# Placing the three turns of a weight conversion within a pair of attention heads

## The chip, the cores and the metric

The kernel runs on one core of a Trainium2 chip. Its time is the device time of one execution in microseconds (us). Before the change it is 1604.77 us, the median of three runs (1603.15 to 1604.81).

## What is computed

The program is an attention layer with normalised queries and keys, followed by a gated feed-forward layer. Cut to what matters:

```python
# q, k, v: (8 sequences, 12 heads, 448 positions, 64); float32
rmsnorm = lambda x, g: x / sqrt(mean(x*x, -1) + 1e-6) * g
scores  = 1/8 * rmsnorm(q, g_q) @ rmsnorm(k, g_k).T
attn    = softmax(scores)
x       = (attn @ v), heads side by side            # (3584, 768)
xn      = x / sqrt(mean(x*x, -1) + 1e-6) * rms_g
out     = (silu(xn @ w_gate) * (xn @ w_val)) @ w_out   # weights float64 -> float32
```

The three weight matrices arrive as float64 and have to become float32 on the chip, in 72 pieces. That is the conversion which the change is about.

## The kernel before

Heads are worked on in pairs: 6 pairs to a sequence (`NPAIR`), 48 in all (`NG`). Each engine runs its own instructions in the order in which the program states them. `pe(fn)` states one step of TensorE work and then whatever was put off with `after(n, ...)` until `n` such steps later. So the place of a call in the text is its place in every engine's stream.

Pair 0 and pairs 1 to 6 (`g <= NPAIR`) run alone, before there is any feed-forward work to lie beside. In these, the parts concerned are:

```python
raw_pool, cv_pool = pool("c_raw", 7), pool("c_cv", 4)
ps_s, ps_m, ps_f = 4, 1 and 3 banks of PSUM
...
def squares(g, i):                      # sums of squares of q (i = 0) or k (i = 1)
    nc.scalar.activation(sq, st["qk", g][:, i], ACT.Square)              # L478
    after(1, reduce)                    # VectorE tensor_reduce            L481
    ...
    elif i == 1:
        after(2, lambda: rms_qk(g))     # GpSimd add, pow                  L497, L498
        after(2, lambda: norm_q(g))     # GpSimd multiply x2               L503

def turn(g, i):                         # transposes of q (i = 0) or k (i = 1)
    ...                                 # TensorE                          L519, L523
    if i == 0:
        nc.scalar.activation(st["qT", g], ps, ACT.Copy, scale=gqk)        # L524
        nc.vector.tensor_copy(st["kT", g][:, LAST], ps[:, S:])            # L525
    else:
        nc.vector.tensor_copy(st["kT", g][:, FULL], ps[:, FULL])          # L527

def score(g, cs):                       # for each chunk c and head j
    ps = ps_s.tile(...); nc.tensor.matmul(ps, kT, qT)                     # L537
    nc.scalar.activation(e, ps, ACT.Exp, scale=rs)                        # L541

def rests(g):                           # the last 64 positions
    nc.tensor.matmul(...)               # scores of pair g                 L567
    av = ps_m.tile(...)                 # the only bank of ps_m
    nc.tensor.matmul(av, ...)           # values of pair g-1, first term   L573
    nc.tensor.matmul(den, ones, e)      # denominators of g-1, first term  L578
    nc.scalar.activation(e, ps, ACT.Exp)                                  # L582

def values(g):  nc.tensor.matmul(av, vt, e)      # 6 of them               L589

def sums(g):
    nc.tensor.matmul(den, ones, e)      # 6 of them                        L602
    nc.vector.reciprocal(rd, den)                                         # L606
    nc.vector.tensor_tensor(x, av, rd, ALU.mult)                          # L617
    ...                                 # later: ScalarE square L620/L622, GpSimd sum L623
```

The conversion moves one step on with each call of `convert()`, a turn. One turn works on several pieces at different stages, with `n` the number of the turn:

```python
def convert():
    ...
    if 0 <= n - 5 < len(pieces):        # last stage of piece n-5
        nc.gpsimd.tensor_tensor(w, top, lo, ALU.add)                      # L773
    if 0 <= n - 4 < len(pieces):        # join of piece n-4: three on VectorE
        nc.vector.tensor_scalar(top, top, 122879.99, 2.0**-15, ...)       # L734
        nc.vector.tensor_scalar(top, top, 3, 0x3FFFFFF8, ...)             # L735
        nc.vector.scalar_tensor_tensor(top, hi, -(2**30), top, ...)       # L736
    if 0 <= n - 3 < len(pieces):        # split of piece n-3: two on ScalarE
        top = cv_pool.tile(...)         # one of 4 buffers
        nc.scalar.activation(top, hi, ACT.Abs)                            # L728
        nc.scalar.activation(lo, lo, ACT.Copy, scale=2.0**-29)            # L729
    if n < len(pieces):                 # load of piece n into one of 7 raw buffers
        st["raw", n] = load_raw(pieces[n][1])                             # L719
    if 0 <= n - 7 < len(pieces):        # piece n-7 is put away in DRAM
        keep(pieces[n - 7][0])                                            # L761
```

A `top` buffer is written by the split (L728) and read for the last time by the GpSimd addition (L773) of the same piece, two turns later.

Of the kernel before, what the change touches and what calls it, by code (L numbers as in the profile page):

```python
# [22 lines left out]
NPAIR = H // 2  # L23
# [312 lines left out]
def safe_scores(  # L336
# [45 lines left out]
    def pe(fn):  # L382
        now["t"] += 1
        fn()
        for item in [d for d in due if d[0] <= now["t"]]:
            due.remove(item)
            item[1]()
# [15 lines left out]
    def load_pair(g):  # L403

        if g >= NG:
            return
        b, hp = divmod(g, NPAIR)
        qk = st["qk", g] = qk_pool.tile([128, 2, 2 * NK * D], F32, name="qk")
        nc.sync.dma_start(out=qk[:, 0].rearrange("p (h n) -> p h n", h=2),
                          in_=q[b, 2 * hp:2 * hp + 2, FULL].rearrange("h (p t) d -> p h (t d)", t=NK))  # L410
        for h in range(2):
            nc.sync.dma_start(out=qk[:, 1].rearrange("p (t h d) -> p h t d", h=2, d=D)[:, 1 - h],
                              in_=k[b, 2 * hp + h, FULL].rearrange("(p t) d -> p t d", t=NK))

    def load_v(g):
        if g >= NG:
            return
        b, hp = divmod(g, NPAIR)
        vt = st["v", g] = v_pool.tile([128, 2, NK, D], F32, name="vt")
        nc.sync.dma_start(out=vt.rearrange("p h t d -> p h (t d)"),  # L420
                          in_=v[b, 2 * hp:2 * hp + 2, FULL].rearrange("h (p t) d -> p h (t d)", t=NK))


    def load_rests(b, i, engine):
        if b >= B:
            return
        if i == 0:
            st["rest", b] = rest_pool.tile([128, NPAIR, 2, D], F32, name="rest")
        for h in range(2):
            engine.dma_start(out=st["rest", b][own(i), :, 1 - h], in_=(q, k)[i][b, h::2, LAST].rearrange("h i d -> i h d"))  # L430

    def load_v_rests(b):
        if b >= B:
            return
        vr = st["vr", b] = rest_pool.tile([128, NPAIR, D], F32, name="vr")
        for h in range(2):
            nc.sync.dma_start(out=vr[across(h)], in_=v[b, h::2, LAST].rearrange("h i d -> i h d"))
# [91 lines left out]
    def score(g, cs):  # L529

        qT, kT, rs = st["qT", g], st["kT", g], st["rs", g]
        sc = {}
        for c in cs:
            for j in range(2):
                r = across(j)
                ps = sc[c, j] = ps_s.tile([128, 512], F32, name="sc", tag="s")
                nc.tensor.matmul(ps[:, 0:S], lhsT=kT[r, c * 128:(c + 1) * 128], rhs=qT[r, :], start=True, stop=True)  # L537
        for (c, j), ps in sc.items():
            e = st["e", g, c, j] = e_pool.tile([128, S], F32, name="e")
            n = 2 * NK + c * 2 + 1 - j  # L540
            nc.scalar.activation(e, ps[:, 0:S], ACT.Exp, scale=rs[:, n:n + 1])  # L541


        def first():
            for j in range(2):
                es = st["es", g, j] = tmp.tile([128, S], F32, name="es", tag="es", bufs=4)
                nc.gpsimd.tensor_tensor(es, st["e", g, 0, j], st["e", g, 1, j], ALU.add)  # L547

        def more(of):
            for j in range(2):  # L550
                r = across(j) if of == "rest" else slice(0, 128)
                e = st["e", g, of] if of == "rest" else st["e", g, of, j]
                es = st["es", g, j]
                nc.gpsimd.tensor_tensor(es[r], es[r], e[r], ALU.add)  # L554

        if NK - 1 in cs and not direct(g):
            n = 3 if g == NPAIR + 1 else 2
            after(n, first)
            after(n + 2, lambda: more(2))
            after(n + 3, lambda: more("rest"))  # L560
# [202 lines left out]
    def convert():  # L763

        n = turn_of["n"]
        if n >= TURNS or not room(1):
            return False
        turn_of["n"] += 1
        if 0 <= n - 5 < len(pieces):
            key = pieces[n - 5][0]  # L770
            st[key] = block()
            lo, top = st.pop(("cv", n - 5))
            nc.gpsimd.tensor_tensor(data(key).bitcast(I32), top, lo, ALU.add)  # L773
        if 0 <= n - 4 < len(pieces):
            st["cv", n - 4] = join(*st.pop(("cv", n - 4)))
        if 0 <= n - 3 < len(pieces):
            st["cv", n - 3] = split(st.pop(("raw", n - 3)))
        if n < len(pieces):
            st["raw", n] = load_raw(pieces[n][1])
        if 0 <= n - 7 < len(pieces):  # L780
            keep(pieces[n - 7][0])
        if turn_of["n"] == TURNS:

            free_w.extend(cv_pool.tile([128, BW], F32, name="top") for _ in range(2))
            whole = [raw_pool.tile([128, 2 * BW], F32, name="raw") for _ in range(7)]
            room_so.extend(whole[:6])
            homes = [whole[6][:, 0:BW], whole[6][:, BW:]] + [cv_pool.tile([128, BW], F32, name="top") for _ in range(2)]
            carried.extend(t[:, i * 128:(i + 1) * 128] for t in homes for i in range(3))
        return True
# [421 lines left out]
    def load_rows():  # L1211
        nc.sync.dma_start(out=rg, in_=moe_rms_g.rearrange("(c p) -> p c", p=128))
        nc.sync.dma_start(out=row[:, 0, :], in_=g_q.rearrange("(o d) -> o d", o=1))
        nc.sync.dma_start(out=row[:, 1, :], in_=g_k.rearrange("(o d) -> o d", o=1))
# [20 lines left out]
    def turns(n):  # L1235

        for _ in range(n):
            convert()
# [14 lines left out]
    for g in range(NG + 1):  # L1253
        b, hp = divmod(g, NPAIR)
        if g:
            load_pair(g + 3)
        if hp == 2:
            for i in range(2):
                load_rests(b + 1, i, nc.sync)
            load_v_rests(b + 1)  # L1260
        if g == 0:
            pe(lambda: score(0, (0,)))
            pe(lambda: rests(0))
            pe(lambda: score(0, (1, 2)))
            pe(lambda: turn(1, 0))
            squares(2, 0)
            squares(2, 1)
            pe(lambda: turn(1, 1))
            norm_rests(0, 2, 4)
            for _ in range(3):  # L1270
                convert()
            load_pair(3)
            load_v(2)
            convert()
            load_rows()
            continue
        if g <= NPAIR:
            pe(lambda: score(g, (0,)))
            squares(g + 2, 0)
            squares(g + 2, 1)  # L1280
            turns(g < NPAIR)
            if g > 1:
                pe(lambda: turn(g + 1, 0))
                some_rests(g)
                pe(lambda: turn(g + 1, 1))
            pe(lambda: rests(g))
            pe(lambda: values(g - 1))
            if g == 1:
                pe(lambda: turn(g + 1, 0))
                some_rests(g)  # L1290
                pe(lambda: turn(g + 1, 1))
            load_v(g + 2)
            turns(g < NPAIR)
            pe(lambda: sums(g - 1))
            pe(lambda: score(g, (1, 2)))
            turns(1 if g < NPAIR else 3)
            if g == 2:
                bound()
            continue

        pe(lambda: (rests(g), score(g, (0,)) if g < NG else None))
        if g == NPAIR + 1:
            pe(lambda: rms_x(0))
        pe(lambda: values(g - 1))
        load_v(g + 2)
        if g == NPAIR + 1:
            pe(lambda: score(g, (1,)))
            pe(lambda: norm_x(0))
            pe(lambda: score(g, (2,)))
        pe(lambda: sums(g - 1))  # L1310
        if g == NPAIR + 1:
            begin(0, 15)
        elif g < NG:
            pe(lambda: score(g, (1, 2)))
        st["block"] = now["t"]
        if hp:
            fill()
            squares(g + 2, 0)
            squares(g + 2, 1)
            pe(lambda: turn(g + 1, 0))  # L1320
            some_rests(g)
            fill()
            pe(lambda: turn(g + 1, 1))
            fill()
            continue
        fill(3)
        pe(lambda: turn(g + 1, 0))
        fill(1)
        pe(lambda: rms_x(b - 1))
        squares(g + 2, 0)  # L1330
        squares(g + 2, 1)
        pe(lambda: turn(g + 1, 1))
        fill(len(todo))
        begin(b - 1, 16)
        pe(lambda: norm_x(b - 1))
        fill()
# [41 lines left out]
```

## Time and profile before

| | before |
|---|---|
| time, median of 3 | 1604.77 us |
| span of the profiled execution | 1601.2 us |
| TensorE busy | 1574.3 us (98%) |
| VectorE busy | 879.0 us (55%) |
| ScalarE busy | 469.9 us (29%) |
| GpSimd busy | 658.7 us (41%) |

In the profile PE is TensorE, DVE VectorE, ACT ScalarE, POOL GpSimd and SP the engine that issues the transfers. L773 is line 773 of the kernel. The busy share of TensorE takes in time in which a matrix product was issued and waited in the pipeline, so it is not a measure of how near the engine is to its peak. A row of the timeline gives the start in us from the start of the span, the duration in us, the engine, line and operation, what is written and read, the count, and in square brackets how long the engine stood idle before it and what ended that. The duration of one instruction runs a little past the start of the next on the same engine; where a stream is without gaps, the time that an instruction takes up is the distance between starts.

The pairs that run alone fill about the first 100 us of the span; the conversion lasts until 280 us.

### The profile page before, as it was taken

The numbers are of one execution on the slowest core, as the hardware profiler recorded it, in microseconds if no ns is written. First come the engines' busy times: TensorE is split into PE (matmuls) and PEld (weight loads), VectorE is DVE, ScalarE is ACT, GpSimd is POOL, SyncE is SP. The second block draws the span as 40 slices with busy tenths as digits, with TensorE's granted clock in tenths as the row PEclk, the third lists the DMA queues.
The fourth block names the chain that finished last, engine by engine and source line by source line (L and its number), as shares of the span: only waits on it lengthen the run. The fifth ranks groups of instructions, "written<-read, shape, count | busy, mean of one in ns | idle before, by whom it ended". The sixth has DMA issues, their size and how long they took to land.

```text
span 1601.2 us, 21577 instructions
## 1 busy us (share of the span) xinstructions
PE 1574.3 (98%) x7286; PEld 1115.9 (70%) x7286; DVE 879.0 (55%) x1553; ACT 469.9 (29%) x940; POOL 658.7 (41%) x715
## 2 busy tenths in 40 slices
PE   8999999999999999999999999999999999999998
PEld 4344445687756887568875788667885688859974
DVE  5989899578833566325562354635563355513531
ACT  6746464232222222222222222323322222101010
POOL 7867877465324443343433443344542342000000
PEclk9999999999999999999999999999999999999999
DMA  7648574856756554465544655584554544457552
GB/s 218 197 139 264 164 248 127 280 193 225 234 173 191 154 148 139 133 200 155 151 126 134 207 157 154 148 258 132 162 150 123 172 140 137 124 165 220 174 150 58
DMA packets 261996, 273.28 MB, mean 171 GB/s; under 512 B 78836, under 2 KB 258804, under 8 KB 261876
## 3 DMA queue, kind: packets, MB, share of 16 engines
q1 hardware_dynamic: 260948, 271.61, 56.1%
q8 instruction: 60, 0.98, 0.3%
q14 instruction: 60, 0.49, 0.1%
q10 hardware_dynamic: 800, 0.20, 0.1%
q0 software_dynamic: 128, 0.00, 0.0%
HBM read 232.40 MB, written 39.32 MB: 170 GB/s over the span
## 4 chain that ended last, share of the span: by engine, by line
PE 81%; DVE 5%; POOL 0%; issue 0%; DMA 0%; ACT 0%; SPq 0%; DVEq 0%; POOLq 0%
PE ff L889 40%; PE ff L1079 22%; PE sc L537 6%; PE av L589 5%; PE sc L567 2%; PE den L602 2%; PE tr L519 1%; PE ff L989 1%; DVE top L735 1%; DVE top L736 1%; DVE top L734 0%; PE ff L1107 0%; DVE rd L610 0%; DVE h L912 0%; DVE h L911 0%
## 5 line engine op out<-in xcount | busy, mean ns | idle before, releaser
L889 PE MATMUL ff<-x,w 128*128 128x224 f32 x1878 | 383.2, 355 | 4.4 <-DVE h L912 2.6
L889 PEld LDWEIGHTS ff<-x,w 128*128 128x128 f32 x1878 | 352.5, 191 | 20.2 <-issue 11.1
L547 POOL TENSOR_TENSOR es<-e 128x448 f32<-128x448 f32 x82 | 91.6, 1139 | 497.1 <-ACT e L541 497.1
L889 PE MATMUL ff<-xs,w 128*128 128x224 f32 x1374 | 281.7, 353 | 3.3 <-DVE w L846 3.3
L889 PEld LDWEIGHTS ff<-xs,w 128*128 128x128 f32 x1374 | 258.1, 190 | 7.1 <-issue 6.0
L554 POOL TENSOR_TENSOR es<-es,e 64x448 f32<-64x448 f32 (+1 forms) x164 | 191.8, 1180 | 6.3
L610 DVE RECIPROCAL rd<-rd 128x448 f32<-128x448 f32 x41 | 121.0, 2952 | 110.0 <-ACT rd L609 109.9
L541 ACT ACTIVATE e<-sc,rs 128x448 f32<-128x448 f32 x288 | 161.6, 634 | 47.9 <-PE sc L537 45.6
L1079 PE MATMUL ff<-w,h 128*128 128x384 f32 x498 | 167.8, 487 | 0.6 <-ACT p L1058 0.6
L1079 PE MATMUL ff<-w,raw 128*128 128x384 f32 x468 | 159.5, 487 | 0.3 <-DVE y L1051 0.3
L537 PE MATMUL sc<-qT,kT 64*128 64x448 f32 x576 | 138.4, 572 | 3.3 <-ACT sq L478 1.8
L1079 PEld LDWEIGHTS ff<-w,h 128*128 128x128 f32 x498 | 93.5, 190 | 64.5 <-issue 1.3
L1079 PEld LDWEIGHTS ff<-w,raw 128*128 128x128 f32 x468 | 87.6, 190 | 60.9 <-issue 2.6
L589 PE MATMUL av<-e,vt 128*64 128x448 f32 x576 | 118.8, 548 | 0.0
L498 POOL TENSOR_TENSOR rs<-ms,mhalf 128x12 f32<-128x12 f32 (+1 forms) x50 | 114.2, 2283 | 4.2
L537 PEld LDWEIGHTS sc<-qT,kT 64*128 64x128 f32 x576 | 54.4, 185 | 84.3 <-issue 68.3
L1107 PE MATMUL ff<-x,w 128*128 128x448 f32 x288 | 111.8, 541 | 0.0
L901 DVE TENSOR_TENSOR cc<-ff,u 128x448 f32<-128x448 f32 x84 | 52.3, 623 | 91.8 <-PE ff L889 91.6
L773 POOL TENSOR_TENSOR w<-top,raw 128x384 int32<-128x384 int32 x72 | 77.3, 1087 | 36.5 <-DVE top L736 18.6
L589 PEld LDWEIGHTS av<-e,vt 128*64 128x64 f32 x576 | 37.1, 136 | 75.6 <-issue 74.2
L1107 PEld LDWEIGHTS ff<-x,w 128*128 128x128 f32 x288 | 53.3, 190 | 50.8 <-issue 49.0
L623 POOL TENSOR_TENSOR ss<-ss,rd 128x448 f32<-128x448 f32 x40 | 46.8, 1171 | 79.5 <-ACT rd L622 79.5
(127 smaller groups left out, 1810.0 us busy)
## 6 DMA issues: line engine op xcount, KB each, us to landing
w<-kept SPq DMA_DIRECT2D x511, 192.0 KB, 2.6
w<-kept_o SPq DMA_DIRECT2D x296, 192.0 KB, 2.8
kept<-w SPq DMA_DIRECT2D x89, 192.0 KB, 3.8
qk<-in_q_dram SPq DMA_DIRECT2D x48, 192.0 KB, 3.0
qk<-in_k_dram SPq DMA_DIRECT2D x96, 96.0 KB, 3.2
vt<-in_v_dram SPq DMA_DIRECT2D x48, 192.0 KB, 2.5
raw<-in_moe_w_gate_dram SPq DMA_DIRECT2D x24, 384.0 KB, 4.1
raw<-in_moe_w_val_dram SPq DMA_DIRECT2D x24, 384.0 KB, 4.6
```

Of the source, the lines that this page charges most:

```text
L498: nc.gpsimd.tensor_tensor(st["rs", g][:, cols], ms, mhalf[:, cols], ALU.pow)
L537: nc.tensor.matmul(ps[:, 0:S], lhsT=kT[r, c * 128:(c + 1) * 128], rhs=qT[r, :], start=True, stop=True)
L541: nc.scalar.activation(e, ps[:, 0:S], ACT.Exp, scale=rs[:, n:n + 1])
L547: nc.gpsimd.tensor_tensor(es, st["e", g, 0, j], st["e", g, 1, j], ALU.add)
L554: nc.gpsimd.tensor_tensor(es[r], es[r], e[r], ALU.add)
L589: nc.tensor.matmul(av[own(j), 0:S], lhsT=vt[:, j, c], rhs=st["e", g, c, j], start=False, stop=(c == NK - 1), skip_group_check=True)
L610: nc.vector.reciprocal(rd, rd)
L773: nc.gpsimd.tensor_tensor(data(key).bitcast(I32), top, lo, ALU.add)
L889: nc.tensor.matmul(bank[:, w * HT:(w + 1) * HT], lhsT=wt[:, c * 128:(c + 1) * 128], rhs=x[:, c, :], start=onto is None and w == c == 0, st ...
L901: nc.vector.tensor_tensor(add[name], ps[:, 0:S], add[other], ALU.add)
L1079: nc.tensor.matmul(ps, lhsT=left_o(b, which, LEFT_O[name], c), rhs=data(("wo", b, name, c)), start=first and c == 0, stop=c == NFP - 1, sk ...
L1107: nc.tensor.matmul(bank[w][:, 0:S], lhsT=data(key)[:, c * 128:(c + 1) * 128], rhs=st["x", 0, half][:, c, :], start=half == c == 0, stop=ha ...
```

## The change

Each of the pairs 1 to 5 has three turns of the conversion. Before, one stood behind the sums of squares, one ahead of the denominators (`sums`) and one behind the scores. Now all three stand together, behind the sums of squares and the transposes and ahead of the denominators. The aim is that the nine VectorE instructions of the three joins run while GpSimd is in its chain for the root (L497, L498), and that GpSimd's three additions run while VectorE is in the reciprocal (L606), which reads PSUM. Pair 6 (`g == NPAIR`) has its three turns behind the scores in both versions.

```diff
             pe(lambda: score(g, (0,)))
             squares(g + 2, 0)
             squares(g + 2, 1)
-            turns(g < NPAIR)
             if g > 1:
                 pe(lambda: turn(g + 1, 0))
                 some_rests(g)
@@
                 some_rests(g)
                 pe(lambda: turn(g + 1, 1))
             load_v(g + 2)
-            turns(g < NPAIR)
+
+            turns(3 if g < NPAIR else 0)
             pe(lambda: sums(g - 1))
             pe(lambda: score(g, (1, 2)))
-            turns(1 if g < NPAIR else 3)
+            turns(3 if g == NPAIR else 0)
             if g == 2:
                 bound()
```

`some_rests` normalises a batch of last positions in pairs 1, 3 and 4 and none in pairs 2 and 5; on GpSimd that is L453, L454 and L458, behind L503.

## The prediction

> **What bounds the kernel now.** I read the busy time by stretch first, one stretch for each pair from one reciprocal (L606) to the next. The columns are the stretch, its length, then for PE, PEld, DVE, ACT and POOL the busy us with the count, clock, DMA share and GB/s.
>
> ```profile
> 37.98:48.96 10.98, 10.98 (x61) 4.36 (x59) 10.67 (x21) 8.76 (x18) 8.29 (x9) 1.00 0.74 233
> 48.96:61.78 12.82, 12.43 (x62) 4.92 (x58) 12.58 (x18) 9.45 (x20) 10.86 (x12) 1.00 0.73 222
> 61.78:74.14 12.36, 11.97 (x58) 4.69 (x58) 12.12 (x17) 8.81 (x19) 10.39 (x12) 1.00 0.59 181
> ```
>
> A pair takes 11 to 13 us and VectorE is busy in 97 to 98% of it: it is the bound of these pairs, with TensorE close behind. TensorE needs 10.45 us for a pair where it runs without a gap (the denominators start at 35.27 and at 45.72), so 10.45 is the floor. Next I looked at why VectorE takes 12.8 us; its timeline from 50 us:
>
> ```profile
> 52.87 0.87 DVE L735 TENSOR_SCALAR top<-top 128x384 int32<-128x384 int32 x1
> 53.77 1.25 DVE L736 SCALAR_TENSOR_TENSOR top<-raw,top 128x384 int32<-128x384 int32 x1
> 54.95 1.18 DVE L734 TENSOR_SCALAR top<-top 128x384 f32<-128x384 f32 x1
> ...
> 60.53 0.34 DVE L734 TENSOR_SCALAR top<-top 128x384 f32<-128x384 f32 x1
> 60.91 0.36 DVE L735 TENSOR_SCALAR top<-top 128x384 int32<-128x384 int32 x1
> 61.30 0.56 DVE L736 SCALAR_TENSOR_TENSOR top<-raw,top 128x384 int32<-128x384 int32 x1
> 61.78 2.95 DVE L606 RECIPROCAL rd<-den 128x448 f32<-128x448 f32 x1
> ```
>
> The join at 60.53 takes 1.25 us from start to start. The two joins from 52.48 to 58.55 take 6.07 us instead of 2.5. GpSimd's timeline tells what lies beside them:
>
> ```profile
> 46.95 0.25 POOL L497 TENSOR_SCALAR ms<-ms 128x12 f32<-128x12 f32 x1
> 47.28 2.30 POOL L498 TENSOR_TENSOR rs<-ms,mhalf 128x12 f32<-128x12 f32 x1
> 49.66 0.97 POOL L503 TENSOR_TENSOR qn<-qk,rs 128x192 f32<-128x192 f32 x2
> 50.72 0.25 POOL L453 TENSOR_SCALAR msr<-msr 128x6 f32<-128x6 f32 x1
> 51.05 1.35 POOL L454 TENSOR_TENSOR msr<-msr,mhalf 128x6 f32<-128x6 f32 x1
> 52.48 1.03 POOL L458 TENSOR_TENSOR rest<-rest,msr 128x384 f32<-128x384 f32 x1
> 53.48 3.52 POOL L773 TENSOR_TENSOR w<-top,raw 128x384 int32<-128x384 int32 x3
> ```
>
> The slow joins lie beside L458 and the three L773; the fast one at 60.5 lies beside the root L498. That is the loss the change goes after: about 3.5 us in pairs 3 and 4, 1 to 2 in the others. Last, the timeline of ScalarE and who waits for the additions:
>
> ```profile
> 53.13 0.98 ACT L478 ACTIVATE sq<-qk 128x384 f32<-128x384 f32 x2
> 54.64 0.57 ACT L728 ACTIVATE top<-raw 128x384 f32<-128x384 f32 x1 [0.53 <-POOL w L773]
> 55.11 0.56 ACT L729 ACTIVATE raw<-raw 128x384 int32<-128x384 uint32 x1
> ...
> 67.45 0.57 ACT L728 ACTIVATE top<-raw 128x384 f32<-128x384 f32 x1 [1.47 <-POOL w L773]
> ```
>
> The split begins at 54.64, as the first of the three additions ends. So splits already wait for GpSimd to give a `top` buffer back; as yet it costs 0.5 to 1.5 us that ScalarE can spare.
>
> **What the Trainium skill says.** "SBUF — State Buffer", section "SBUF: two separate sides": VectorE in a two-port mode or with two SBUF inputs, and GpSimd, take a shared port pair in turn as an exclusive lock, and the loser blocks for the whole instruction. The trace agrees: L735 takes 0.36 us alone and 1.06 beside an L773 of 1.0. "PSUM — Partial Sum Buffer", section "Engine vs sequencer instructions": the queues of ScalarE, VectorE and GpSimd are strict FIFO; in the trace nothing overtakes the waiting split at 67.45. "Perfetto Trace Analysis", section "Optimization Strategy": a gap that repeats can mean that buffers for the next tile are missing. The repeated wait of L728 for L773 (34.7 us in 12 waits over the whole run) is of that kind.
>
> **The change part by part.** Nothing is added or removed; TensorE's stream is the same in both builds.
>
> *Gain.* VectorE's joins now run from the end of L481, beside L497 and L498 (2.7 us) and L503; the additions fall beside L606 and L617 (3.6 us), which read PSUM. Unhindered, VectorE needs 2.97 (L606) + 0.55 (L617) + 0.93 (L481 x2) + 0.6 (L525, L527) + 0.46 (L448) + 3 x 1.26 = 9.3 us a pair. VectorE would no longer be the bound. Down to TensorE's floor, the pairs could gain 0.5 + 2.4 + 1.9 us: about 5 us at most.
>
> *Cost: a buffer.* There are four `top` buffers. The split in turn n (piece n-3) takes the buffer of piece n-7, whose addition stands in turn n-2. Before, a pair's turns were a, b, c, and the addition of a stood ahead of L497 in GpSimd's stream; the split of c waited for it without harm. Now all three additions stand behind L497, L498, L503 (and L453 to L458). The third split waits for the first addition of the *same* pair, and in ScalarE's stream the six exponentials (L541) of the next scores stand behind this split. With no more than four score banks, TensorE cannot go on either. This closes a ring that no stretch of idle VectorE time opens:
>
> exponentials 6 x 0.53 = 3.2; squares L478 0.9; L524 0.5; L622 0.46; GpSimd L623 1.2 (it stands ahead of L497); L497 0.33; L498 2.38; L503 1.05; in pairs 3 and 4 L453 to L458 2.75; first L773 1.0; third split 0.9; some 0.15 for hand-overs. Sum: 12.1 us in pairs 2 and 5, 14.8 us in pairs 3 and 4. The exponentials before start at 38.68, 49.13, 61.06, 72.90 and 85.26: periods of 10.45, 11.93, 11.84 and 12.36.
>
> *Laid out by pair.* Pair 1 has no reused buffer; its reciprocal comes two joins later (27.4 to 30.2), the values product of the next pair waits for L617 as `ps_m` has one bank, and after 0.8 + 0.85 + 2.3 + 2.36 us of TensorE work the second reciprocal starts near 40.0 (before 37.98) and pair 2's exponentials near 41.0 (before 38.68): +2.4. Pair 3: 41.0 + 14.8 = 55.8 (before 49.13). Pair 4: 70.6 (61.06). Pair 5: 82.7 (72.90). From there TensorE runs to pair 5's denominators unhindered: first exponential 0.55, two scores 1.1, transposes 0.9, then 0.5 + 0.8 + 0.85 + 2.3 + 2.36, near 92.0 (before 84.3), and pair 6's exponentials start near 93.0 against 85.26: +7.8. Locks between the third join and L503 may add 0.1 to 0.3 in a pair; I take +8.0. Pair 6 and all behind it have the order of before; everything there is chained to these pairs, so I let the 8.0 stand to the end: 1604.8 + 8.0 = 1612.8.
>
> **The rivals.** (1) *The lock goes and the buffer does not matter*: the third split finds its buffer in time. For it: the change is made for this and VectorE is at 98%. Against it: L498 alone takes 2.4 us ahead of the addition. The time would be 1600 to 1602. (2) *Both cancel*: the wait shows but the time saved at VectorE, or slack up to 280 us (ScalarE waits for L773 there for 32.7 us anyway), takes it back: 1604 to 1607. Against it: VectorE and GpSimd are chained to each other through that whole stage and have nothing they could do earlier. (3) *The reciprocal alone*: only the later L606 and the single `ps_m` bank count, a ring of 9.9 us, below TensorE's floor: +2 us, 1607.
>
> **Range and chances.** My ring gives +8, with 2 us either way from durations and locks; rival 3 is the low side, an L503 that waits for the lock twice in each pair the high one. The range is 1606.5 to 1617. Two per cent would be 32 us, a third of all the time these pairs take: 0.01 for faster, 0.98 for the same, 0.01 for slower.
>
> **What would show it.** In the profile after: L728 waiting for L773 once in each of pairs 2 to 5, some 18 us together (3.2, 5.8, 5.9, 3.7); the L541 behind it starting near 41, 56, 71 and 83 us; L606 near 30, 40, 52, 67, 81 and 92; joins at 1.3 us and VectorE with idle time before L525; the L773 beside L606. I am wrong if the third split of a pair starts ahead of L498's end, or if the shift at 92 us is gone by 280.

## The result and the profile after

| | before | after |
|---|---|---|
| time, median | 1603.96 us (4 runs) | 1614.27 us (4 runs) |
| ratio to before, 95% interval | | 1.0063 (1.0046 to 1.0081) |
| span of the profiled execution | 1601.2 us | 1612.8 us |
| VectorE busy | 879.0 us | 870.2 us |

The change makes the kernel 10.3 us slower. VectorE is busy for 8.8 us less all the same, so what the change is for does happen.

One thing has to be known for reading times off the two traces: in some executions TensorE is granted about half its clock for a few us during pair 0, near 400 us, or both, and each such stretch costs some 1.6 us. The profiled execution before has only the second, the one after both. Between 12 and 14 us the granted clock is 1.00 before and 0.50 after, and pair 1's denominators start at 24.77 before and at 26.38 after. The change does not touch pair 0, and in e9 below, which has the changed order, the clock there is 1.00. So 1.6 us come off the starts after pair 0 in the profile after, and of the 11.6 us between the spans, 10.0 belong to the change.

Busy time by stretch in the kernel after, from one pair's first exponential to the next pair's (pairs 2, 3 and 4; columns as before: length, then PE, PEld, DVE, ACT and POOL busy with counts, granted clock, DMA share, GB/s):

```profile
43.13:58.27 15.14, 11.12 (x59) 4.14 (x55) 12.53 (x21) 8.70 (x19) 10.54 (x12) 1.00 0.68 214
58.27:73.92 15.65, 11.97 (x55) 4.95 (x55) 9.49 (x16) 8.93 (x19) 10.57 (x12) 0.89 0.50 151
73.92:86.38 12.46, 11.79 (x55) 4.88 (x55) 6.62 (x14) 8.32 (x18) 8.10 (x10) 0.86 0.47 136
```

No engine fills its stretch any more: in the second one VectorE is busy for 9.5 of 15.65 us and GpSimd for 10.6. Time that no engine fills is waiting, and a ring of waits is what the prediction named. Follow one turn of it, in pair 4. First VectorE's timeline, from the third join on:

```profile
67.87 0.35 DVE L734 TENSOR_SCALAR top<-top 128x384 f32<-128x384 f32 x1
68.25 0.55 DVE L735 TENSOR_SCALAR top<-top 128x384 int32<-128x384 int32 x1
68.83 0.74 DVE L736 SCALAR_TENSOR_TENSOR top<-raw,top 128x384 int32<-128x384 int32 x1
69.50 2.94 DVE L606 RECIPROCAL rd<-den 128x448 f32<-128x448 f32 x1
...
78.54 0.22 DVE L525 COPY kT<-tr 128x64 f32<-128x64 f32 x1 [5.43 <-ACT qT L524]
```

The join takes 1.6 us here, a little of it beside L503, and others 1.26; none takes 3. Then VectorE stands idle for 5.43 us. GpSimd's timeline of the same pair:

```profile
63.88 1.14 POOL L623 TENSOR_TENSOR ss<-ss,rd 128x448 f32<-128x448 f32 x1 [4.59 <-ACT rd L622]
65.10 0.24 POOL L497 TENSOR_SCALAR ms<-ms 128x12 f32<-128x12 f32 x1
65.43 2.44 POOL L498 TENSOR_TENSOR rs<-ms,mhalf 128x12 f32<-128x12 f32 x1
67.94 1.22 POOL L503 TENSOR_TENSOR qn<-qk,rs 128x192 f32<-128x192 f32 x2
...
71.99 2.95 POOL L773 TENSOR_TENSOR w<-top,raw 128x384 int32<-128x384 int32 x3
```

The additions L773 take 0.98 us each, with no join beside them; but the first cannot start before 71.99. Beside the reciprocal, as intended, lies only the start of the first one here; behind it VectorE has L617 (72.48) and then nothing to do. In pair 3 it is the same (L773 at 56.34, the reciprocal from 53.85); in pairs 2 and 5, without L453 to L458, the additions lie largely beside the reciprocal (84.43 and 85.11 in pair 5). ScalarE's timeline shows who waits for the first addition:

```profile
66.36 0.56 ACT L729 ACTIVATE raw<-raw 128x384 int32<-128x384 uint32 x1
73.03 0.56 ACT L728 ACTIVATE top<-raw 128x384 f32<-128x384 f32 x1 [6.11 <-POOL w L773]
73.49 0.53 ACT L729 ACTIVATE raw<-raw 128x384 int32<-128x384 uint32 x1
73.92 3.23 ACT L541 ACTIVATE e<-sc,rs 128x448 f32<-128x448 f32 x6
77.02 0.96 ACT L478 ACTIVATE sq<-qk 128x384 f32<-128x384 f32 x2
77.85 0.66 ACT L524 ACTIVATE qT<-tr,gqk 128x448 f32<-128x448 f32 x1
```

The second split ends at 66.9. The third is held for 6.11 us, until the addition at 71.99 has given its `top` buffer back, and the six exponentials go right behind it. TensorE, with all four score banks full, stands still meanwhile:

```profile
69.14 1.77 PE L537 MATMUL sc<-qT,kT 64*128 64x448 f32 x8
74.59 1.54 PE L537 MATMUL sc<-qT,kT 64*128 64x448 f32 x4 [3.68 <-ACT e L541]
```

L524 at 77.85 then lets VectorE go on at 78.54, and the squares of L478 feed the next root. Such waits of a third split are 3.69, 6.11, 6.11 and 3.72 us long in pairs 2 to 5.

### The profile page after: what moved, and what is told of

It reads as the page before. It is cut to its first block, busy times and chain, and to the rows that moved or that the text cites. A ratio compares the mean times of both kernels' runs of the same rounds, so it can differ in the third digit from the quotient of the medians.

```text
span 1612.8 us, 21581 instructions
## 1 busy us (share of the span) xinstructions
PE 1576.6 (98%) x7286; PEld 1116.0 (69%) x7286; DVE 870.2 (54%) x1553; ACT 470.3 (29%) x940; POOL 659.2 (41%) x715
## 4 chain that ended last, share of the span: by engine, by line
PE 80%; DVE 5%; issue 1%; POOL 0%; DMA 0%; ACT 0%; SPq 0%; DVEq 0%; POOLq 0%
PE ff L889 39%; PE ff L1079 22%; PE sc L537 6%; PE av L589 5%; PE sc L567 2%; PE den L602 2%; PE tr L519 1%; PE ff L989 1%; DVE top L735 1%; DVE top L736 1%; DVE top L734 0%; PE ff L1107 0%; DVE h L912 0%; DVE h L911 0%; DVE rd L610 0%
## 5 line engine op out<-in xcount | busy, mean ns | idle before, releaser
L541 ACT ACTIVATE e<-sc,rs 128x448 f32<-128x448 f32 x288 | 161.1, 633 | 41.3 <-PE sc L537 38.6
L498 POOL TENSOR_TENSOR rs<-ms,mhalf 128x12 f32<-128x12 f32 (+1 forms) x50 | 114.3, 2287 | 4.2
L773 POOL TENSOR_TENSOR w<-top,raw 128x384 int32<-128x384 int32 x72 | 76.3, 1074 | 34.3 <-DVE top L736 20.8
L623 POOL TENSOR_TENSOR ss<-ss,rd 128x448 f32<-128x448 f32 x40 | 46.5, 1163 | 95.3 <-ACT rd L622 95.3
```

The costliest lines, as they stand in the source:

```text
L498: nc.gpsimd.tensor_tensor(st["rs", g][:, cols], ms, mhalf[:, cols], ALU.pow)
```

## The experiments

Ratios are to the kernel before, measured beside it, with 95% intervals. One per mille is 1.6 us. Versions are to be compared by the ratio, not by the median. All edits but e2's are shown against the changed kernel.

| version | median us | ratio |
|---|---|---|
| changed kernel | 1614.27 | 1.0063 (1.0046 to 1.0081) |
| e1: it, with a fifth top buffer | 1602.67 | 0.9999 (0.9991 to 1.0008) |
| e2: before, with a fifth top buffer | 1602.89 | 1.0000 (0.9992 to 1.0009) |
| e3: only the third turn moved | 1601.10 | 0.9986 (0.9979 to 0.9993) |
| e4: only the first turn moved | 1604.34 | 1.0007 (0.9998 to 1.0015) |
| e5: e3 with a fifth buffer | 1599.65 | 0.9983 (0.9976 to 0.9989) |
| e6: e3 from pair 2 on | 1600.48 | 0.9983 (0.9977 to 0.9990) |
| e7: e1 from pair 2 on | 1599.42 | 0.9982 (0.9975 to 0.9988) |
| e8: changed kernel from pair 2 on | 1613.16 | 1.0063 (1.0050 to 1.0077) |
| e9: changed kernel, root twice | 1618.43 | 1.0093 (1.0078 to 1.0109) |
| e10: e1, root twice | 1602.96 | 1.0001 (0.9993 to 1.0010) |
| e11: e6 with a fifth buffer | 1600.55 | 0.9978 (0.9970 to 0.9985) |

### e1 and e2: one buffer more

The fifth buffer is the last of the weight slots, which is not in use during these pairs; of the first 16 pieces, every fifth takes it.

```diff
+    spare = free_w[-1]
-    def split(raw):
+    def split(raw, p):
@@
-        top = cv_pool.tile([128, BW], I32, name="top")
+        top = spare[:, 0:BW].bitcast(I32) if p < 16 and p % 5 == 4 else cv_pool.tile([128, BW], I32, name="top")
@@
-            st["cv", n - 3] = split(st.pop(("raw", n - 3)))
+            st["cv", n - 3] = split(st.pop(("raw", n - 3)), n - 3)
```

In the changed kernel:

> The changed kernel with a fifth top buffer in pairs 1 to 5 (a weight slot that is not in use so early), nothing else. Theory (ring through the buffer that a pair's third split waits for): the third split needs an addition of the pair before, the ring is gone, pairs run at TensorE's floor of about 10.5 us, the exponentials of pair 6 start some 2 us ahead of the kernel before, the time is 1601 to 1603, 11 to 13 below the changed kernel. Rival (three joins ahead of the reciprocal, with the one bank of ps_m, cost the time): no more than 2 us of the 10 come back, 1612 or more.

In the kernel before:

> The kernel before with the same fifth top buffer. Theory: its splits waited 0.5 to 1.5 us and off the path, so the time stays within 1 us of the kernel before (1603 to 1605). Rival (a fifth buffer helps any order): it gains as much as the changed kernel does with it, 5 us or more.

With the buffer the changed kernel's loss of 10 us is gone; the kernel before stays as it was. In e1's ScalarE timeline no split of these pairs waits for L773, and the exponentials wait for TensorE instead:

```profile
61.67 0.58 ACT L728 ACTIVATE top<-raw 128x384 f32<-128x384 f32 x1
62.13 0.58 ACT L729 ACTIVATE raw<-raw 128x384 int32<-128x384 uint32 x1
65.02 3.26 ACT L541 ACTIVATE e<-sc,rs 128x448 f32<-128x448 f32 x6 [2.32 <-PE sc L537]
```

In its stretches for pairs 2 to 5 TensorE is hardly ever idle; two of them have the length that the prediction gave as the floor:

```profile
43.15:53.60 10.45, 10.45 (x57) 4.15 (x55) 8.72 (x19) 8.74 (x19) 6.08 (x7) 1.00 0.73 234
53.60:65.02 11.42, 11.40 (x57) 4.41 (x55) 10.46 (x18) 8.76 (x18) 10.87 (x12) 1.00 0.69 205
65.02:75.47 10.45, 10.45 (x57) 4.15 (x56) 8.44 (x16) 8.23 (x17) 10.04 (x11) 1.00 0.69 205
75.47:86.38 10.91, 10.91 (x57) 4.42 (x56) 5.84 (x7) 5.50 (x12) 7.81 (x9) 1.00 0.76 240
```

The other two are longer by 1.0 and 0.5 us, which the busy time of TensorE hides. The first values term (L573) otherwise runs side by side with the scores of L567, both in 0.81 us (46.22 to 47.03). In the longer stretch it comes behind them, and both take 1.76 us:

```profile
56.67 0.97 PE L567 MATMUL sc<-qT,kT 64*64 64x448 f32 x4
57.66 0.97 PE L573 MATMUL av<-e,vr 64*64 64x448 f32 x4
58.43 0.95 PE L578 MATMUL den<-e,ones 64*64 64x448 f32 x4
```

L573 needs the one bank of `ps_m`, and L617 is done with it at 57.5. So a reciprocal that comes behind three joins, which is rival 3's point, still costs something here.

The version was expected to start pair 6's exponentials 2 us ahead of the kernel before. Pair 0 has the half clock here too and costs 1.7 us (pair 1's denominators start at 26.48); less that, they start at 84.7 against 85.26, only 0.6 ahead. Pair 2's still start 2.8 us late (43.15, less 1.7, against 38.68), which e7 takes up.

### e3 and e4: each half alone

```diff
 # e3: the turn behind the squares stays, the one behind the scores moves
+            turns(g < NPAIR)
@@
-            turns(3 if g < NPAIR else 0)
+            turns(2 if g < NPAIR else 0)
 # e4: the turn behind the squares moves, the one behind the scores stays
-            turns(3 if g < NPAIR else 0)
+            turns(2 if g < NPAIR else 0)
@@
-            turns(3 if g == NPAIR else 0)
+            turns(1 if g < NPAIR else 3)
```

> One half of the change: the turn behind the scores goes ahead of the denominators, the turn behind the sums of squares stays (1, 2 and 0 turns). Theory: the first addition of a pair stands ahead of the root in GpSimd's stream, so the third split doesn't wait for the root, no ring: 1601 to 1604. Rival (fewer than all three together is no matter, the late reciprocal costs): 1608 or more.

> The other half: the turn behind the sums of squares goes ahead of the denominators, the one behind the scores stays (0, 2 and 1 turns). Theory: the third split waits for the root again but stands behind four of the six exponentials, so the ring is some 2 us shorter in each pair (10 and 12.7 us): 1604 to 1608. Rival (late reciprocal): about half of the 10 us in both halves, 1608 to 1610 here as in the other half.

Neither half has the loss: e3 is a gain of 2.2 us, e4 lies within its noise of the kernel before (in its trace pair 6's exponentials start 1.2 us late, the half clock of pair 0 taken off). It takes both: moving the first turn puts the first addition behind the root, and moving the third puts all six exponentials behind the split that waits for it. In e4's ScalarE timeline the split still waits, but four exponentials of the pair are out by then:

```profile
52.58 2.21 ACT L541 ACTIVATE e<-sc,rs 128x448 f32<-128x448 f32 x4 [1.34 <-PE sc L537]
57.03 0.56 ACT L728 ACTIVATE top<-raw 128x384 f32<-128x384 f32 x1 [2.24 <-POOL w L773]
...
57.94 1.14 ACT L541 ACTIVATE e<-sc,rs 128x448 f32<-128x448 f32 x2
```

### e9 and e10: a known time put on the ring

```diff
-        nc.gpsimd.tensor_tensor(st["rs", g][:, cols], ms, mhalf[:, cols], ALU.pow)
+        for _ in range(2 if g in (4, 7) else 1): nc.gpsimd.tensor_tensor(st["rs", g][:, cols], ms, mhalf[:, cols], ALU.pow)
```

`g` is the pair whose root is taken, two ahead of the pair in work: these are the roots in pairs 2 and 5.

> The changed kernel with the root (L498, 2.4 us from start to start) computed twice in pairs 2 and 5, the second time onto the same result. Theory (GpSimd's chain is on the ring): every added us comes out at the end, 2 x 2.4 = 4.8 us over the changed kernel, 1617 to 1620. Rival (the loss comes from VectorE or TensorE and GpSimd has time to spare in these two pairs, busy some 8 of 12.5 us): under 1.5 us more.

> The same doubled roots in the changed kernel with the fifth top buffer. Theory: without the ring GpSimd has about 2 us to spare in pairs 2 and 5, so 0 to 2 us over the version with the buffer alone: 1601 to 1605. If GpSimd's chain reaches the end by another way: 4 us or more.

In the changed kernel the ratio goes from 1.0063 to 1.0093, 3.0 per mille or 4.8 us for 2 x 2.4 us put in; with intervals of some 2.5 us either way that agrees with one for one and does not prove it. In e9's trace the third splits of pairs 2 and 5 wait longer by 1.9 and 1.5 us than in the kernel after:

```profile
42.56 0.55 ACT L728 ACTIVATE top<-raw 128x384 f32<-128x384 f32 x1 [5.59 <-POOL w L773]
...
88.36 0.55 ACT L728 ACTIVATE top<-raw 128x384 f32<-128x384 f32 x1 [5.24 <-POOL w L773]
```

The round from pair 1's exponentials to pair 2's is 15.16 us (28.30 to 43.46) where the kernel after has 13.29 (29.84 to 43.13), and that from pair 4's to pair 5's 14.97 (74.28 to 89.25) where it has 12.46: 1.9 and 2.5 us more. That is not the root alone. GpSimd's timeline of pair 2 in e9:

```profile
35.57 4.95 POOL L498 TENSOR_TENSOR rs<-ms,mhalf 128x12 f32<-128x12 f32 x2
40.60 0.97 POOL L503 TENSOR_TENSOR qn<-qk,rs 128x192 f32<-128x192 f32 x2
41.53 2.94 POOL L773 TENSOR_TENSOR w<-top,raw 128x384 int32<-128x384 int32 x3
```

The second root takes up 2.5 us, but L503 and the first L773 no longer lie beside the third join and give back 0.6, so that 1.9 reach the split. In pair 5 it is 2.0 in the same way; the other 0.5 come from the six exponentials ahead, which take 3.6 us (74.28 to 77.91) in place of 3.1 (73.92 to 77.02) as they wait for TensorE's scores. So what reaches the third split comes out at the next exponentials in full, but a root's 2.4 us reach it only as 1.9 to 2.0. From pair 1's exponentials to pair 6's it is 73.0 us (28.30 to 101.32) against 67.0 in the kernel after (29.84 to 96.80): 6.1 us more in all, as the round from pair 5 to pair 6 is 1.65 us longer too. TensorE's clock is 0.50 from 92 to 94 us in e9 and 1.00 in the kernel after.

With the fifth buffer the same roots cost nothing that is seen (0.9999 and 1.0001), and in the traces pair 6's exponentials follow pair 2's by 43.1 us in e10 (43.30 to 86.40) and 43.2 in e1. In these two pairs GpSimd's chain reaches the end only by way of the buffer.

### e8 and e7: the first reciprocal

Pair 1 has its turns as in the kernel before, pairs 2 to 5 have theirs together; e8 has four buffers, e7 five.

```diff
+            turns(g == 1)
@@
-            turns(3 if g < NPAIR else 0)
+            turns(3 * (g < NPAIR) - 2 * (g == 1))
@@
-            turns(3 if g == NPAIR else 0)
+            turns(3 * (g == NPAIR) + (g == 1))
```

> The three turns together from pair 2 on, pair 1 as in the kernel before, four top buffers. Theory (ring): pair 2's third split waits for GpSimd's chain all the same and sets its exponentials, so nothing comes back: 1612 to 1615. Rival (the late first reciprocal is 2 us or more of the loss): 1611 or less.

> The three turns together from pair 2 on, pair 1 as in the kernel before, with the fifth top buffer. Theory: with no ring the late first reciprocal is what is left of the cost (the second product of values waited 1.8 us for it); a join less ahead of it gives back about 1 us: 1601 to 1602. If the late reciprocal costs all of the 2.8 us by which pair 2's exponentials were late: below 1600.

With four buffers nothing is seen to come back, by ratios with intervals of some 2 to 3 us either way; the trace is finer. In e8 pair 2's third split waits all the same:

```profile
42.41 0.55 ACT L728 ACTIVATE top<-raw 128x384 f32<-128x384 f32 x1 [3.94 <-POOL w L773]
```

The exponentials behind it start at 43.30; less 2.0 us (pair 1's denominators start at 26.75 there) that is 41.3, where the kernel after has 41.5. The late first reciprocal is hidden under the ring.

With five buffers it is worth 1.7 per mille, 2.7 us, more than the 1 us that I expected; the other case that I had named came true. In e7 pair 2's exponentials start at 40.30, less 1.6 as early as in the kernel before. I had taken TensorE's idle time of 1.8 us for the cost. But L567 and L573, which otherwise run side by side in 0.81 us, take 3.58 in e1 (33.01 to 36.59), 2.8 more; in e7 they take 0.81 again (32.92 to 33.73). And I had counted one join less ahead of the first reciprocal, where two fewer stand: it starts at 29.02 in e7 and at 32.12 in e1. So e7 is what the change was for: 2.9 us (1.9 to 4.0) less than before.

### e5, e6 and e11: the half that helps, with each of these

> Only the third turn moved (1, 2 and 0 turns), with the fifth top buffer. With four buffers this order's splits still waited 0.3 and 1.0 us for an addition in pairs 4 and 5. Theory: those waits are all that the buffer can give here: 0 to 1 us less than without it, 1600 to 1601. Rival (a buffer is worth as much in every order as in the changed kernel): 5 us or more less.

> Only the third turn moved, from pair 2 on; pair 1 has its turns as in the kernel before. Theory: pair 1's first reciprocal no longer comes a join later, but pair 2's then has one join more ahead of it, so most of the delay only moves on: 0.3 to 1.2 us less than with pair 1 moved too, 1600 to 1601.

> Only the third turn moved, from pair 2 on, with the fifth top buffer: all that helped one by one. The parts gave 2.1, about 0.5 and about 0.5 us: 1599 to 1601 expected, no clear gain over the three turns together with the buffer from pair 2 on, since TensorE's 10.45 us a pair bounds both.

The edits are those of e3, of the buffer, and of pair 1. Each point estimate lies 0.3 to 0.5 per mille below the version without it, inside the intervals of both. The fastest by ratio is e11, 3.5 us (2.4 to 4.8) ahead of the kernel before; it is not told apart from e7. The prediction gave 5 us as the most that these pairs could gain.

## Why the prediction was right, and where its sizes were off

**The ring.** Shown: the waiting split, the exponentials behind it and TensorE's full banks stand in the trace in the order predicted, one buffer takes the loss away, and a root's 2.4 us put on GpSimd's chain reaches the third split as 1.9 to 2.0 and lengthens the round by that. 18.6 us of waits in pairs 2 to 5 were predicted; 19.6 were seen.

**Its sizes.** The exponentials of pairs 2 to 6 were predicted to start near 41.0, 55.8, 70.6, 82.7 and 93.0. Less 1.6 they start at 41.5, 56.7, 72.3, 84.8 and 95.2. The sum falls short by 2.2 us, in three places. In pair 2 I let the exponentials start as TensorE's scores were there (41.0). In the trace the third split begins at 42.20, less 1.6 at 40.6, and takes 0.9 us of ScalarE ahead of them: 0.5 us. Each turn of the ring takes 0.3 to 0.4 us more than my sum: L503 beside a join takes up 1.3 for my 1.05, L623 starts 0.67 us behind the start of L622, for which I had 0.46, L498 takes up 2.5 for 2.38, and the exponentials a little less than I had. And in the round from pair 3's exponentials to pair 4's the six took 3.6 us (58.27 to 61.89) in place of 3.1, as the last scores came late at TensorE's lower clock, which is told below.

**The reciprocal of pair 1.** It was late as predicted (32.03, less 1.6, is 30.4; predicted 30.2), and so was the next (42.12, less 1.6, is 40.5; predicted 40.0). But I counted +2.4 us for it and set the ring on top. e8 shows that the ring alone is enough in pair 2 too: without the late reciprocal the split waits for 3.94 us, and pair 2's exponentials start only 0.2 us earlier. Either cause alone makes them late by about as much (2.6 us in e8, 2.8 in e1). That the two are so nearly equal, so that counting one of them gave nearly the right number for pair 2 (2.4 for 2.8), was luck.

**The gain.** I had the additions fall beside L606 and L617. In pairs 3 and 4 they come too late for most of that; L453 to L458 stand ahead of them.

**To the end.** The shift at pair 6's exponentials is 96.80 - 85.26 = 11.5 us, that of the spans 11.6. Nothing was given back, which is against rival 2.

**The rivals.** The first one, that the lock goes and the buffer does not matter, is half right: the lock goes, but the third split does not find its buffer, and the three turns together gain only with a buffer to spare (e7). The third, the reciprocal alone, is what is left of the cost in e1 and not the cost of the change.

## What to carry to other kernels

Putting work together on one engine to keep it from another's way also moves each of its stages on all engines; write down which instruction gives back the buffer that the last of the group takes, and what stands ahead of it in its own engine's stream. If the way from there leads through an instruction that the group itself holds up, there is a ring, and its length is the time of a round whatever the busy shares say. One buffer more, for the time that the group is together, opens it. So does leaving one stage of the group where it was: e6, with four buffers, is not told apart from e7 with five (0.9983 and 0.9982).

## What was not expected

A wait of TensorE can cost more than its length. In the kernel after, it stands idle for 4.67 us ahead of 58.94, and the clock that it is granted then falls; stretches of 2 us, the clock being the third number from the end:

```profile
60.00:62.00 2.00, 2.00 (x7) 0.75 (x5) 0.00 (x0) 1.73 (x4) 0.00 (x0) 0.50 1.05 321
62.00:64.00 2.00, 2.00 (x15) 1.09 (x15) 0.63 (x3) 1.80 (x4) 0.12 (x1) 0.84 0.07 15
...
76.00:78.00 2.00, 2.00 (x12) 1.49 (x15) 0.00 (x0) 2.00 (x6) 0.00 (x0) 0.57 0.90 257
78.00:80.00 2.00, 2.00 (x12) 0.47 (x4) 1.46 (x4) 1.59 (x4) 0.95 (x1) 0.58 0.00 1
```

Three transposes that take 0.55 us at 45.25 took 0.90 at 61.25, and three that take 0.49 at 45.74 took 0.85 at 76.80. In e1, which has no such gaps, the clock is 1.00 in each of the four stretches shown. The Trainium skill has this in "TensorE: Matmul & The Clock Gate", section "Part 1: The HAM clock gate (the "warmup" mystery)": the array goes to half its clock after an idle window of some 3.4 us. These two gaps agree with it: 4.67 us was followed by 0.50, and 3.68 us by 0.57. Other traces here do not: in e8 gaps of 2.58 us (ahead of 43.97) and 2.20 us (ahead of 74.78) were followed by 0.50 too, and gaps of the same 1.85 us near 402 us by 0.52 in the kernel before and by 1.00 in e1. The measurement decides: shorter gaps can do it as well, and what decides whether they do is not shown.

The root L498 takes 2.4 us on GpSimd, and joins beside it run at full speed (0.35, 0.36 and 0.56 us in the kernel after, from 66.61 on), where an L773 of 1.0 us holds each up (1.18, 1.06 and 1.38 us in the kernel before, from 54.95 on). The Trainium skill ("SBUF — State Buffer", section "SBUF: two separate sides") has a GpSimd operation hold the shared pair for its whole length; here the measurement decides, and for L498 that does not hold. L498 has 12 elements to a partition and L773 has 384. That the few elements are the reason was not tried.
